# The opening of a fused convolution and SwiGLU kernel: one operation for the taps' second part, late passes one chunk earlier, other places for loads

## The chip, the cores and the metric

The kernel runs on one core of one Trainium2 chip. The metric is the device time of one execution in microseconds (us), the median of three runs. All other times are us from the start of the profiled span unless they are marked ns. Engines are named as in the profile: PE (TensorE, matmuls; PEld are its weight loads), DVE (VectorE), ACT (ScalarE), POOL (GpSimd), SP (SyncE, whose queue issues most transfers). A small q behind an engine's name marks its sequencer, which issues transfers.

## The reference

A causal convolution over the sequence, 7 taps for each of 8 heads (the taps are a softmax of `weight`), then a SwiGLU block on its result. Everything is float32 in and out.

```python
B, S, D = 8, 4096, 192          # x; H = 8 heads of 24 channels, K = 7 taps, Dff = 1536
w = exp(weight - max(weight, -1)); w = w / (sum(w, -1) + 1e-9)
conv[b, s, h, :] = sum over k of w[h, k] * x_padded[b, s + k, h, :]     # 6 zeros ahead
g   = conv @ w_gate             # 192 x 1536
val = conv @ w_val              # 192 x 1536
out = (g * sigmoid(g) * val) @ w_out        # 1536 x 192
```

## The kernel before

**Tiling.** The 32768 tokens are 64 blocks of 512 tokens (`TB`); two blocks make a pair, 32 pairs in all. A block goes through the SwiGLU part in 12 chunks of 128 hidden columns (`NCH`). A chunk's first half is 3 steps of 2 matmuls: `gate` on the lower 64 rows of the array (line 558), `val` on the upper 64 rows (559), side by side. Then ACT makes silu of `gate` (563) and DVE multiplies it with `val` to h (565). PSUM holds two buffers of gate (chunk 2 of block 0 uses a third, the buffer called run), and three of val, so val of chunk j waits for h of chunk j-3. The second half, `acc` += h times w_out (570), lags one block: its matmuls stand between the first halves of the next block, 4 or 6 units of two matmuls a chunk. Chunks are counted through: block 0 has chunks 0 to 11, block 1 has 12 to 23, pair 1 begins at chunk 24.

**The convolution of pair 1 and later** is done by ACT, DVE and POOL in three groups a pair: group 0 (channels 0 to 127 of the first block), group 1 (channels 128 to 191 of both blocks), group 2 (channels 0 to 127 of the second block). Each group's steps have places by chunk: `turn`, DVE's transposition (line 114, squares sqA or sqB to xtA or xtB); `start`, ACT's first product into PSUM (`run`, 485); `acts`, ACT products (478); `dves`, DVE multiply-and-add (495, the last gives aD); `pool`, POOL products (500) and sums (507); `join`, the sum of all parts to xc (513); `swap`, two transfers that exchange the halves of xc to xs (461, 462). A chunk reads xc and xs. A step of a place stands, on every engine's queue, behind that chunk's own work. Engines work their queues strictly in that order. `PLAN["opening"]` (line 17) gives these places for pair 1 as (turn, start, acts, dves, pool, join, swap), one tuple a group.

**The convolution of pair 0** is done by PE, as matmuls of x with banded matrices. The taps are made first: line 273 is the exponential, `turned` the rotated taps, `norm` the reciprocal of their sum. `left` holds the normed taps as two float16 parts: part 0 is rounded (289), part 1 is what the rounding left (292: the taps in float32 as `full`; 293: `full` minus part 0). Four matmuls (337: hiA, loA, hiC, loC) repeat the two parts over the rows, DVE cuts them to bands T (345). x is cast to float16 by ACT (windows 0 to 2) and POOL (windows 3 to 5) at line 244. Then block 0 is convolved (361), folded (420 to 424), gathered (414) and copied to three operands D0, D1, D2 (427 to 431), one for each of a chunk's three steps. Block 1 is convolved in three late passes of 48 matmuls, put between the chunks of block 0: `lateA(0)`, `lateA(1)` and `lateC`. They read x16p, which POOL casts at line 247. Their results go to foldA1 and foldC1 by ACT and are exchanged by transfers (669) to swapA1 and swapC1; block 1 (chunk 12 and on) reads all of them. `spread_taps` (435 to 439) puts the taps, in three parts that POOL makes (lines 323 to 327), on the partitions for the other engines (wn); it uses the masks `mask` and `own`.

**Queues.** POOL's queue issues the weight transfers w_sb in three lots (chunks 0 to 3, 4 to 7, 8 to 11), gate and val apart (169), between its other work. SP's queue takes the taps, x, the squares (103), the exchanges, the swaps and the output (600), in program order; an instruction that waits holds all behind it. `mark` (455) puts an empty instruction on SP's queue that waits for a matmul, and a later matmul waits for it.

**Places of the loads of squares.** `emit_load(q, part, half)`: parts 2 and 3 are sqB, parts 0 and 1 sqA. For pair 1, sqA comes in two halves at chunks 5 and 9; for pair 2 the parts come at chunks 16 (part 2), 17 (part 3), 20 (part 0) and 22 (part 1).

Of the kernel before, what the change touches and what calls it, by code (L numbers as in the profile page):

```python
# [15 lines left out]
    load=((2, -47), (3, -40), (0, -34), (1, -28)),  # L16
    opening=(
# [3 lines left out]
    ),  # L21
    gate=2, val=3, lead=4, third=(2,),
# [4 lines left out]
def kernel(  # L27
# [9 lines left out]
    nc = tc.nc  # L37
    fp32 = mybir.dt.float32
    fp16 = mybir.dt.float16
    int32 = mybir.dt.int32  # L40
    AF = mybir.ActivationFunctionType
    ALU = mybir.AluOpType
    AX = mybir.AxisListType

    B, S, D = x.shape
    H, K = weight.shape
    NT = B * S
    Dff = moe_w_gate.shape[1]
    P = 128
    DB = D - P  # L50
# [12 lines left out]
    const_pool = ctx.enter_context(tc.tile_pool(name="const", bufs=1))  # L63
# [63 lines left out]
    HALF, STEP, W, NW = TB // 2, 85, 96, 6  # L127
    ROWS, LOADED = 94, 96
# [14 lines left out]
    RT = 8 * H  # L143
    taps = const_pool.tile([H, K], fp32, tag="taps", name="taps")
    nc.sync.dma_start(out=taps, in_=weight)
    x_sb = xpool.tile([P, 2, NW, D], fp32, tag="x_sb", name="x_sb", bufs=1)
# [49 lines left out]
    def where(out, t, bits):  # L196
# [16 lines left out]
        out=plain, in_=plain, pattern=[[-32, 4], [-1, grp]],  # L213
# [5 lines left out]
    mask = const_pool.tile([RT, D], fp16, tag="mask", name="mask")  # L219
    nc.gpsimd.memset(mask, 0.0)  # L220
    nc.gpsimd.affine_select(
        out=mask[:, :].rearrange("r (h c) -> r h c", h=H),
# [1 line left out]
        pattern=[[-8, H], [0, grp]],  # L224
        compare_op=ALU.not_equal, fill=1.0, base=0, channel_multiplier=1,
    )
    own = const_pool.tile([RT, P], fp16, tag="own", name="own")
    nc.gpsimd.tensor_copy(
        own[:, :].rearrange("h (t c) -> h t c", t=2),
        mask[:, P:D].unsqueeze(1).to_broadcast([RT, 2, DB]),  # L230
    )
    load_w(0, 4, 0)
    load_w(0, 4, 1)

# [1 line left out]
    x16 = xpool.tile([P, NW, D + 8], fp16, tag="x16", name="x16", bufs=1)  # L236
# [4 lines left out]
        return t.rearrange("p n (h t c) -> p n h t c", t=2, c=grp)[:, :, :, e, :]  # L241

    def cast(copy, lo, hi):
        copy(x16[0:ROWS, lo:hi, 0:D], x_sb[0:ROWS, 0, lo:hi, :])

    def cast_parity(copy, e):
        copy(parity(x16p[0:ROWS, e, :, :], e), parity(x_sb[0:ROWS, 1, :, :], e))


    wmax, wsum, norm = (const_pool.tile([RT, 1], fp32, tag=n, name=n) for n in ("wmax", "wsum", "norm"))  # L250
# [29 lines left out]
    nc.vector.reciprocal(norm, wsum)  # L280

    REP = -(-ROWS // 8)
    full = const_pool.tile([RT, 8], fp32, tag="full", name="full")
    left = const_pool.tile([RT, 2, REP, 8], fp16, tag="left", name="left")

    def repeated(t):
        return t[:, :].unsqueeze(1).to_broadcast([RT, REP, 8])
# [1 line left out]
    nc.vector.tensor_tensor(  # L289
        left[:, 0, :, :], repeated(turned), norm.unsqueeze(1).to_broadcast([RT, REP, 8]), op=ALU.mult  # L290
    )
    nc.vector.tensor_tensor(full, turned, norm.to_broadcast([RT, 8]), op=ALU.mult)
    nc.vector.tensor_tensor(left[:, 1, :, :], repeated(full), left[:, 0, :, :], op=ALU.subtract)
    left = left[:, :, :, :].rearrange("r i n m -> r i (n m)")

    sync_after(nc.sync.nop(), spinning, "block 1's x behind the first weights")
# [4 lines left out]
            emit_load(1, part, None)  # L301
    nc.scalar.activation(two, one, AF.Silu)
    cast(nc.scalar.copy, 0, 3)
    cast(nc.gpsimd.tensor_copy, 3, NW)

    def place(k):
        lo, hi, at = ((0, DB, 0), (DB, 96, 0), (0, 32, 32), (32, 96, 0))[k]
        nc.gpsimd.tensor_copy(
            spread[:, k, :, at : at + hi - lo], plain[:, lo:hi].unsqueeze(1).to_broadcast([P, 2, hi - lo])
        )  # L310
# [4 lines left out]
    load_w(4, 8, 1)  # L315
    place(2)
    place(3)
    for b in range(2):
        load_w(8, NCH, b)

    parts = const_pool.tile([RT, 3, K], fp16, tag="parts", name="parts")
    raw, rest = (const_pool.tile([RT, K], fp32, tag=n, name=n) for n in ("raw", "rest"))
    nc.gpsimd.tensor_tensor(raw, soft[:, 0:K], norm.to_broadcast([RT, K]), op=ALU.mult)
    nc.gpsimd.tensor_copy(parts[:, 0, :], raw)
    nc.gpsimd.tensor_tensor(rest, raw, parts[:, 0, :], op=ALU.subtract)
    nc.gpsimd.tensor_copy(parts[:, 1, :], rest)
    nc.gpsimd.tensor_tensor(parts[:, 2, :], rest, parts[:, 1, :], op=ALU.subtract)

# [109 lines left out]

    for e in range(2):
        cast_parity(nc.gpsimd.tensor_copy, e)

    foldA1, swapA1 = (
        const_pool.tile([P, 2, TH], fp16, tag=n, name=n) for n in ("foldA1", "swapA1")
# [181 lines left out]
    def at_chunk(c, f):  # L627
        todo.setdefault(c, []).append(f)
# [33 lines left out]
    def lateA(g):  # L662
        if g == 0:
            late_sum()
        halves(g, late["sum"][:, g, :])
# [20 lines left out]
        at_chunk(2 * NCH, blank)  # L686

    late = {}
    at_chunk(3, lambda: lateA(0))
    at_chunk(4, lambda: spread_taps(tpool.tile([P, TB], fp32, tag="run", name="run")))  # L690
    at_chunk(4, lambda: lateA(1))
    at_chunk(4, outA)
    at_chunk(7, lateC)
    if n_pairs > 1:
        for half, c in enumerate((5, 9)):
            for part in (0, 1):
                at_chunk(c, lambda part=part, half=half: emit_load(1, part, half))

# [3 lines left out]
    for q in range(2, n_pairs):  # L702
        base = 2 * NCH * q
        for part, c in PLAN["load"]:
            c = {2: 16, 3: 17, 0: 20, 1: 22}[part] if q == 2 else base + c
            at_chunk(c, lambda q=q, part=part: emit_load(q, part))
        for g in range(3):
            c = base + PLAN["start"][g]
            plan_group(
                q, g, c + PLAN["turn"], c, [c + o for o in PLAN["acts"][g]],  # L710
                [c + o for o in PLAN["dves"][: 4 - PLAN["npool"][g]]],
                c + PLAN["pool"], c + PLAN["join"],
                c + PLAN["swap"][g],
            )
# [7 lines left out]
    for n in range(2 * n_pairs):  # L722
        block = Block(n)
        for j in range(NCH):
            src, units = before if j < NCH - lead // 4 else block, late_start.get(at, 4)
            if n == 0:
                src, units = block, 0
            elif n == 2 * n_pairs - 1 and src is block:
                units = 0
            los, his = src.second(units)  # L730
            half = src.done // (2 * NCH) - 1 if units and src.done % (2 * NCH) == 0 else None
            if n == 0 and j < 2:
                if j == 0:
                    for k in range(2):
                        for i in range(2):
                            block.first(i, (k,))
                block.first(j, (2,))
            elif half is None:
                block.first(j)
            for lo, hi in zip(los, his):  # L740
                lo()
                hi()
            if half is not None:
                src.evacuate(half)
                block.first(j)
            block.gate(j)
            if half is not None:
                src.store(half)
            for f in todo.pop(at, ()):
                f()  # L750
            at += 1
        before = block
# [61 lines left out]
```

## Time and profile before

| | |
|---|---|
| median of 3 runs | 774.21 us (773.54 to 774.4) |
| the profiled execution | 773.69 us, of which the span from first to last instruction 771.9 us |
| mean granted clock of PE | 0.999 |
| busy share PE, PEld, DVE, ACT, POOL | 99%, 76%, 85%, 86%, 86% |
| instructions | 28286 |
| transfers | 67.28 MB, mean 87 GB/s |

In a row of a timeline stand start, length, engine, line, operation, the output and the input with their shapes, how many instructions are merged in the row, and in brackets how long the engine had been idle before and what ended it. A row of a chain of waits has start, length and the work (or "issue", time in which nothing that the profile shows was waited for). A row of transfers has output and input, the issuing queue, how many, KB each, and us from issue to landing. Matmuls overlap: their lengths are latencies, and the distance of their starts is what they cost PE.

### The profile page before, as it was taken

The numbers are of one execution on the slowest core, as the hardware profiler recorded it, in microseconds if no ns is written. First come the engines' busy times: TensorE is split into PE (matmuls) and PEld (weight loads), VectorE is DVE, ScalarE is ACT, GpSimd is POOL, SyncE is SP. The second block draws the span as 40 slices with busy tenths as digits, with TensorE's granted clock in tenths as the row PEclk, the third lists the DMA queues.
The fourth block names the chain that finished last, engine by engine and source line by source line (L and its number), as shares of the span: only waits on it lengthen the run. The fifth ranks groups of instructions, "written<-read, shape, count | busy, mean of one in ns | idle before, by whom it ended". The sixth has DMA issues, their size and how long they took to land.

```text
span 771.9 us, 28286 instructions
## 1 busy us (share of the span) xinstructions
PE 764.1 (99%) x11035; PEld 588.3 (76%) x11035; DVE 659.2 (85%) x1045; ACT 660.6 (86%) x1188; POOL 667.6 (86%) x654
## 2 busy tenths in 40 slices
PE   8899999999999999999999999999999999999998
PEld 4777777777777777777777777777777777777776
DVE  6888888889888888888888888888888888888875
ACT  6888888888888888888888888888888888888875
POOL 6899988888988889988889888899888899888850
PEclk9999999999999999999999999999999999999999
DMA  9544344433444443444334444334443434444211
GB/s 162 103 85 85 82 97 84 94 86 80 88 87 95 84 86 87 87 88 95 85 79 86 95 84 95 86 83 87 83 98 82 89 85 88 88 90 91 61 47 53
DMA packets 255287, 67.28 MB, mean 87 GB/s; under 512 B 207920, under 2 KB 255152, under 8 KB 255152
## 3 DMA queue, kind: packets, MB, share of 16 engines
q1 hardware_dynamic: 252048, 63.48, 39.3%
q0 software_dynamic: 2800, 1.77, 1.6%
q8 instruction: 86, 1.41, 0.8%
q14 instruction: 49, 0.40, 0.2%
q10 hardware_dynamic: 304, 0.22, 0.1%
HBM read 29.65 MB, written 25.17 MB: 71 GB/s over the span
## 4 chain that ended last, share of the span: by engine, by line
PE 95%; POOL 3%; DVE 1%; issue 1%; DMA 0%; ACT 0%; SPq 0%; POOLq 0%; DVEq 0%; ACTq 0%
PE val L559 49%; PE acc L570 34%; PE gate L558 11%; POOL t L507 1%; POOL t L500 1%; DMA xs<-xc 0%; POOL xc L513 0%; PE acc L765 0%; ACT silu L563 0%; PE D L414 0%; PE idle L264 0%; PE acc L361 0%; PE val L765 0%; PE run L765 0%; PE hiA L361 0%
## 5 line engine op out<-in xcount | busy, mean ns | idle before, releaser
L565 DVE TENSOR_TENSOR h<-silu,val 128x512 f16<-128x512 f16 x768 | 508.8, 679 | 103.7 <-ACT silu L563 74.3
L563 ACT ACTIVATE silu<-gate 128x512 f16<-128x512 f32 x768 | 452.7, 594 | 80.1 <-PE gate L558 73.8
L570 PE MATMUL acc<-wo_sb,h 64*128 64x192 f16 x6048 | 471.7, 243 | 1.0 <-SPq L455 1.0
L507 POOL TENSOR_TENSOR t<-t,t 128x512 f32<-128x512 f32 x310 | 393.3, 1269 | 61.6 <-ACT t L478 39.2
L570 PEld LDWEIGHTS <-h 64*128 64x128 f16 x6048 | 397.2, 94 | 62.9 <-SPq L455 1.3
L558 PE MATMUL gate<-xc,w_sb 64*128 64x512 f16 x1116 | 409.7, 376 | 0.0
L559 PE MATMUL val<-xc,w_sb 64*128 64x512 f16 x1116 | 409.7, 376 | 0.0
L558 PE MATMUL gate<-xs,w_sb 64*128 64x512 f16 x1116 | 360.2, 376 | 0.7 <-DMA xs<-xc 0.7
L559 PE MATMUL val<-xs,w_sb 64*128 64x512 f16 x1116 | 360.0, 376 | 0.4 <-DMA xs<-xc 0.4
L559 PEld LDWEIGHTS <-w_sb 64*128 64x128 f16 x2340 | 212.0, 94 | 105.1 <-issue 3.6
L558 PEld LDWEIGHTS <-w_sb 64*128 64x128 f16 x2340 | 212.1, 94 | 5.1 <-issue 2.3
L513 POOL TENSOR_TENSOR xc<-t,aD 128x512 f16<-128x512 f32 x93 | 118.1, 1270 | 7.3
L500 POOL TENSOR_SCALAR t<-xtA,wn 128x512 f32<-128x512 f32 x155 | 105.7, 692 | 0.0
L478 ACT ACTIVATE t<-xtA,wn 128x512 f32<-128x512 f32 x124 | 88.4, 713 | 0.0
L608 ACT COPY o<-acc 128x384 f32<-128x384 f32 x126 | 60.3, 478 | 19.7 <-PE acc L570 6.5
L500 POOL TENSOR_SCALAR t<-xtB,wn 128x512 f32<-128x512 f32 x62 | 42.1, 691 | 6.4 <-DVE xtB L114 6.4
L495 DVE SCALAR_TENSOR_TENSOR aD<-xtA,wn,run 128x512 f32<-128x512 f32 x62 | 45.9, 740 | 0.0
L478 ACT ACTIVATE t<-xtB,wn 128x512 f32<-128x512 f32 x62 | 44.2, 713 | 0.0
L485 ACT ACTIVATE run<-xtA,wn 128x512 f32<-128x512 f32 x62 | 42.5, 686 | 0.5 <-DVE aD L495 0.5
L114 DVE STREAM_TRANSPOSE xtA<-sqA 128x544 f32<-128x544 f32 (+1 forms) x48 | 34.6, 720 | 0.0
L495 DVE SCALAR_TENSOR_TENSOR run<-xtA,wn,run 128x512 f32<-128x512 f32 x31 | 23.2, 749 | 0.0
L495 DVE SCALAR_TENSOR_TENSOR run<-xtB,wn,run 128x512 f32<-128x512 f32 x31 | 23.2, 748 | 0.0
(111 smaller groups left out, 182.9 us busy)
## 6 DMA issues: line engine op xcount, KB each, us to landing
out_dram<-o SPq DMA_DIRECT2D x127, 192.0 KB, 2.0
sqA<-in_x_dram SPq DMA_DIRECT2D x92, 132.0 KB, 3.1
xs<-xc SPq DMA_DIRECT2D x186, 64.0 KB, 2.0
sqB<-in_x_dram SPq DMA_DIRECT2D x96, 68.0 KB, 2.3
headA<-in_x_dram SPq DMA_DIRECT2D x28, 128.0 KB, 2.7
headB<-in_x_dram SPq DMA_DIRECT2D x14, 68.0 KB, 2.5
headB<-in_x_dram SPq DMA_DIRECT2D x14, 64.0 KB, 2.1
x_sb<-in_x_dram SPq DMA_DIRECT2D x3, 216.0 KB, 3.3
```

Of the source, the lines that this page charges most:

```text
L478: mul(parts[-1], *self.tap(k))
L485: nc.scalar.mul(self.aD, *self.tap(0))
L495: nc.vector.scalar_tensor_tensor(out=self.aD, in0=v, scalar=s, in1=run, op0=ALU.mult, op1=ALU.add)
L500: self.product(k, lambda t, v, s: nc.gpsimd.tensor_scalar(t, v, scalar1=s, scalar2=1.0, op0=ALU.mult, op1=ALU.mult), self.parts)
L507: nc.gpsimd.tensor_tensor(self.parts[0], self.parts[0], t, op=ALU.add)
L513: nc.gpsimd.tensor_tensor(xc, self.parts[0], self.aD, op=ALU.add)
L558: nc.tensor.matmul(g, w[0:DB, ca, f], a[0:DB, :], start=(i == 0), stop=(i == 2))
L559: nc.tensor.matmul(v, w[DB:P, cb, f], b[DB:P, :], start=(i == 0), stop=(i == 2))
L563: nc.scalar.activation(s, self.g.pop(j), AF.Silu)
L565: nc.vector.tensor_tensor(h, s, self.v.pop(j), op=ALU.mult)
L570: ins = nc.tensor.matmul(acc, self.h[j][r, ts(s, P)], wo_r[r, j, :], start=first and j == 0, stop=not first and j == NCH - 1, skip_group_c ...
L608: nc.scalar.copy(self.o[:, 2 * half : 2 * half + 2, :], self.acc[:, :, 0:D])
```

## The change

- The taps' second part: `full` is gone; one scalar_tensor_tensor computes `turned * norm - left[0]`.
- POOL's cast of windows 3 to 5 waits for that operation.
- `own` moves on POOL from ahead of the first weight transfers to behind the last `place`, ahead of the third lot of weights. The five operations that make `parts` move behind POOL's casts of x16p.
- Chunks 0 and 1: the steps on D0 of both chunks still come first; then chunk 0's steps on D1 and D2, then chunk 1's. Before, D1 came for both chunks ahead of D2.
- The late passes stand at chunks 2, 3 and 6 instead of 3, 4 and 7, with the copies and exchanges behind them. `spread_taps` stays at 4.
- Group 1 of pair 1: `start` at chunk 7 instead of 6, the first DVE step at 9 instead of 8.
- Loads of squares: pair 1's sqA first half at chunk 4 instead of 5; pair 2's at 11, 12, 20 and 21 instead of 16, 17, 20 and 22.

No matmul is added or removed; DVE has one operation less.

```diff
-        (5, 6, (9, 12), (8, 12), 6, 13, 16),
+        (5, 7, (9, 12), (9, 12), 6, 13, 16),
...
-    own = const_pool.tile([RT, P], fp16, tag="own", name="own")
-    nc.gpsimd.tensor_copy(
-        own[:, :].rearrange("h (t c) -> h t c", t=2),
-        mask[:, P:D].unsqueeze(1).to_broadcast([RT, 2, DB]),
-    )
     load_w(0, 4, 0)
     load_w(0, 4, 1)
...
-    nc.vector.tensor_tensor(full, turned, norm.to_broadcast([RT, 8]), op=ALU.mult)
-    nc.vector.tensor_tensor(left[:, 1, :, :], repeated(full), left[:, 0, :, :], op=ALU.subtract)
+    left_second = nc.vector.scalar_tensor_tensor(
+        out=left[:, 1, :, :], in0=repeated(turned), scalar=norm, in1=left[:, 0, :, :],
+        op0=ALU.mult, op1=ALU.subtract,
+    )
...
-    cast(nc.gpsimd.tensor_copy, 3, NW)
+    sync_after(cast(nc.gpsimd.tensor_copy, 3, NW), left_second, "not beside the taps")
...
     place(3)
+    own = const_pool.tile([RT, P], fp16, tag="own", name="own")
+    nc.gpsimd.tensor_copy(
+        own[:, :].rearrange("h (t c) -> h t c", t=2),
+        mask[:, P:D].unsqueeze(1).to_broadcast([RT, 2, DB]),
+    )
     for b in range(2):
         load_w(8, NCH, b)
...
     for e in range(2):
         cast_parity(nc.gpsimd.tensor_copy, e)
 
+    parts = const_pool.tile([RT, 3, K], fp16, tag="parts", name="parts")
+    raw, rest = (const_pool.tile([RT, K], fp32, tag=n, name=n) for n in ("raw", "rest"))
+    nc.gpsimd.tensor_tensor(raw, soft[:, 0:K], norm.to_broadcast([RT, K]), op=ALU.mult)
+    nc.gpsimd.tensor_copy(parts[:, 0, :], raw)
+    nc.gpsimd.tensor_tensor(rest, raw, parts[:, 0, :], op=ALU.subtract)
+    nc.gpsimd.tensor_copy(parts[:, 1, :], rest)
+    nc.gpsimd.tensor_tensor(parts[:, 2, :], rest, parts[:, 1, :], op=ALU.subtract)
...
-    at_chunk(3, lambda: lateA(0))
+    at_chunk(2, lambda: lateA(0))
     at_chunk(4, lambda: spread_taps(tpool.tile([P, TB], fp32, tag="run", name="run")))
-    at_chunk(4, lambda: lateA(1))
-    at_chunk(4, outA)
-    at_chunk(7, lateC)
+    at_chunk(3, lambda: lateA(1))
+    at_chunk(3, outA)
+    at_chunk(6, lateC)
     if n_pairs > 1:
-        for half, c in enumerate((5, 9)):
+        for half, c in enumerate((4, 9)):
...
-            c = {2: 16, 3: 17, 0: 20, 1: 22}[part] if q == 2 else base + c
+            c = {2: 11, 3: 12, 0: 20, 1: 21}[part] if q == 2 else base + c
...
                 if j == 0:
-                    for k in range(2):
-                        for i in range(2):
-                            block.first(i, (k,))
-                block.first(j, (2,))
+                    block.first(0, (0,))
+                    block.first(1, (0,))
+                block.first(j, (1, 2))
```

More of the change, by code (lines that the diff above doesn't have):

```diff
@@ L243, in cast @@
     def cast(copy, lo, hi):
-        copy(x16[0:ROWS, lo:hi, 0:D], x_sb[0:ROWS, 0, lo:hi, :])
+        return copy(x16[0:ROWS, lo:hi, 0:D], x_sb[0:ROWS, 0, lo:hi, :])
     def cast_parity(copy, e):
@@ L282 @@
     REP = -(-ROWS // 8)
-    full = const_pool.tile([RT, 8], fp32, tag="full", name="full")
     left = const_pool.tile([RT, 2, REP, 8], fp16, tag="left", name="left")
@@ L317 @@
     place(3)
+    own = const_pool.tile([RT, P], fp16, tag="own", name="own")
[3 more added lines that the diff above has]
+    )
     for b in range(2):
         load_w(8, NCH, b)
[L321 to L327, printed above, removed]
     T = const_pool.tile([P, 2, H, W], fp16, tag="T", name="T")
```

## The prediction

> **What bounds the kernel now.** I read the stages first (busy time of each engine by stretch), then the chain of waits of the first 56 us, then the rows of the opening, engine by engine.
>
> ```profile
> 12.00:14.00 2.00, 1.67 (x42) 0.71 (x42) 1.79 (x3) 1.56 (x4) 0.18 (x1) 1.00 1.30 186
> 18.00:20.00 2.00, 1.54 (x58) 0.84 (x54) 1.30 (x3) 1.51 (x4) 1.36 (x2) 1.00 0.49 88
> 32.00:34.00 2.00, 1.10 (x24) 1.03 (x26) 0.87 (x2) 1.05 (x2) 1.92 (x3) 1.00 0.46 75
> 50.00:690.00 640.00, 640.00 (x9172) 495.93 (x9170) 557.76 (x872) 560.82 (x1010) 579.19 (x549) 1.00 0.42 88
> ```
>
> The columns: stretch, length, then busy us of PE, PEld, DVE, ACT and POOL, granted clock, DMA share, GB/s. From 50 to 690 us PE is never idle, and the change touches nothing there. So it can gain only what it brings forward the moment from which PE is saturated. PE's holes, 0.33 at 12-14, 0.46 at 18-20 and 0.90 at 32-34, lie in the opening. Which of them count is told by the chain of waits (start, length, what):
>
> ```profile
> 17.72 0.75 DVE xtB L114
> 23.75 0.72 ACT t L478
> 24.61 1.27 POOL t L507
> 32.73 1.27 POOL xc L513
> 45.84 3.82 DMA xs<-xc
> ```
>
> POOL works without a hole from 24.61, when ACT's product at chunk 12 (23.75) sets group 1's sum free, to the xc of group 0 at 34.00. Chunk 24, the first of token pair 1, needs that xc and its swapped copy xs. So **the time of chunk 24 is set by POOL, POOL's by chunk 12, and chunk 12's by how fast block 0 (chunks 0 to 11) runs.** Holes of PE in chunks 14 to 23 (32-34) are no gain by themselves. The chain's next step, xs at 45.84, is for chunk 36, a transfer that the change leaves in its place.
>
> **The front (L289 to the first gate matmul).**
>
> ```profile
> 2.87 0.36 POOL L228 COPY own<-mask 64x128 f16<-64x128 f16 x1
> 4.05 0.64 POOL L169 DMA_DIRECT2D w_sb<-in_moe_w_val_dram  x1
> 4.68 0.68 POOL L244 CAST x<-x_sb 94x576 f16<-94x576 f32 x1
> ...
> 3.85 0.25 DVE L289 TENSOR_TENSOR left<-turned,norm 64x96 f16<-64x96 f32 x1
> 4.02 0.61 DVE L292 TENSOR_TENSOR full<-turned,norm 64x8 f32<-64x8 f32 x1
> 4.67 0.80 DVE L293 TENSOR_TENSOR left<-full,left 64x96 f16<-64x96 f32 x1
> ...
> 4.31 0.55 PE L337 MATMUL hiA<-pick,left 64*94 64x384 f16 x1
> 5.53 0.55 PE L337 MATMUL loA<-pick,left 64*94 64x384 f16 x1 [0.67 <-DVE left L293]
> 5.88 0.52 PE L337 MATMUL hiC<-pick,left 64*94 64x384 f16 x1
> 6.65 1.05 PE L361 MATMUL hiA<-T,x 94*32 94x85 f16 x48
> 10.15 0.39 PE L558 MATMUL gate<-D,w_sb 64*128 64x512 f16 x1
> ...
> w_sb<-in_moe_w_val_dram POOLq DMA_DIRECT2D x1, 192.0 KB, 5.5
> ```
>
> Removed: L292 (0.61) and L293 (0.80), done at 5.47. Added: one operation over 64x96 that waits for L289 (4.10). Nearest rows: L289, same size, 0.25; L293, same size beside POOL's cast, 0.80. I take 0.3, since the cast now waits behind it: done at 4.45 (4.94 at the upper end). loA then follows hiA at PE's own pace (5.88-5.53 = 0.35): 4.31+0.35 = 4.66 instead of 5.53, **-0.87** (at the upper end 4.98, -0.55). loA, hiC, loC and the convolution from 6.65 on follow in PE's order and move as much. POOL's cast is not late: it began at 4.68 behind the two weight transfers, and own (0.36), which stood ahead of them, is now behind; with the new wait it begins at about 4.5 (5.0 at the upper end, harmless, since the convolution would begin at 5.8 to 6.1). Queued behind the cast on POOL are place, own and the later weight transfers: they come 0.2 earlier to 0.3 later.
>
> The first gate and val matmuls also need the val weights: 4.05+5.5 = 9.55. Without own ahead they are issued 0.36 earlier, so 9.2, or still 9.55 if the transfer engines were the limit. First matmuls: **10.15 to 9.28** (9.6 at worst).
>
> The Trainium skill ("SBUF — State Buffer", Who interferes with whom) says that a VectorE operation with two SBUF inputs is blocked by a GpSimd operation that reads SBUF, not by one that only writes. L293 agrees: it ends 0.11 after the cast that began with it (5.36). L292, 64x8 and still 0.61, does not: only a transfer's issue (4.05 to 4.69) lies beside it. By the rule the new operation costs about 0.3, by L292's row up to 0.6 more.
>
> **Block 0.**
>
> ```profile
> 10.74 0.37 PE L558 MATMUL gate<-D,w_sb 64*128 64x512 f16 x1
> 10.95 0.37 PE L558 MATMUL gate<-D,w_sb 64*128 64x512 f16 x1
> 12.95 0.37 PE L559 MATMUL val<-D,w_sb 64*128 64x512 f16 x1 [0.33 <-DVE h L565]
> 13.69 0.65 PE L361 MATMUL acc<-T,x16p 94*32 94x85 f16 x48
> 14.27 0.39 PE L558 MATMUL gate<-D,w_sb 64*128 64x512 f16 x1
> 15.63 0.39 PE L558 MATMUL gate<-D,w_sb 64*128 64x512 f16 x1
> 19.75 0.37 PE L558 MATMUL gate<-D,w_sb 64*128 64x512 f16 x1 [0.46 <-ACT silu L563]
> ...
> 11.58 1.57 ACT L563 ACTIVATE silu<-gate 128x512 f16<-128x512 f32 x3 [0.74 <-PE val L559]
> 18.49 0.69 ACT L485 ACTIVATE run<-xtB,wn 128x512 f32<-128x512 f32 x1 [0.76 <-DVE xtB L114]
> ...
> 12.21 2.70 DVE L565 TENSOR_TENSOR h<-silu,val 128x512 f16<-128x512 f16 x4 [1.22 <-ACT silu L563]
> ...
> 9.89 1.26 POOL L247 CAST x16p<-x_sb 94x576 f16<-94x576 f32 x2
> ...
> 4.39 2.64 SPq L103 DMA_DIRECT2D sqB<-in_x_dram  x4
> sqB<-in_x_dram SPq DMA_DIRECT2D x1, 68.0 KB, 8.3
> ```
>
> *Order of chunks 0 and 1.* The matmuls on D1 (10.74 before, about 9.87 now) are followed by those on D2 of chunk 0, not by D1 of chunk 1: silu 0 comes one matmul step earlier. A step is 0.216 (10.74 to 10.95), a chunk three of them, 0.65. Silu 0: 11.58-0.87-0.22 = 10.49, h 0 at 11.12, and val of chunk 3, which waits for h 0 (its PSUM buffer), 12.95 to 11.86.
>
> *Late passes one chunk earlier.* The first (48 matmuls, 14.27-13.69 = 0.58 of PE) stood behind chunk 3 and now falls into the hole ahead of it: from 9.87 seven steps end chunk 2 at 11.38, the pass lies at 11.38-11.96, chunk 3 at 11.96 (from 12.95: -1.0). It needs x16p, cast by 11.15 before; five operations on parts move from ahead of that cast to behind it and only own (0.36) comes ahead, so it is earlier, and even its old time would do. The parts themselves are first wanted by the tap matmuls after chunk 4, some 2.5 later. Chunk 3 (0.65) and the second pass (0.58) put chunk 4 at 13.2 (from 14.27: -1.1); with no pass behind it, only the taps (15.63-14.27-0.65-0.58 = 0.13), chunk 5 is at 13.98 (from 15.63: **-1.7**). VectorE, 0.67 a chunk (12.21, four in 2.70), gets to h 5 at 15.5 and to xtB, whose place at chunk 5 is kept, at 16.15 (from 17.72: **-1.6**). Its input sqB is there: the last of its four loads is issued before 7.03 and lands 8.3 after its issue, so before 15.4.
>
> *ACT's run one chunk later.* Before, ACT stood 0.76 for xtB and then did run (18.49, 0.69) ahead of silu 7 (about 19.1); PE's chunk 9 waited for that (19.75). Now silu 7 is ahead of run: it comes at 16.7, run at 17.2, which xtB (done 16.9) no longer delays. Chunk 9 moves to 17.3 (-2.4). The product that run feeds is one chunk later too (place 8 to 9); it is wanted by aD at chunk 12 only. From there VectorE's 0.67 a chunk and its two extra operations hold the pace: chunk 12 at 20.2, ACT's product at 21.5 (from 23.75: -2.2), POOL's last sums and xc as much. **Block 0 with the front: -2.2 at POOL.**
>
> **Loads and swaps on SP.**
>
> ```profile
> 30.20 2.51 SPq L103 DMA_DIRECT2D sqB<-in_x_dram  x2
> 34.02 0.76 SPq L461 DMA_DIRECT2D xs<-xc  x1
> ...
> 32.90 0.50 PE L570 MATMUL acc<-wo_sb,h 64*128 64x192 f16 x8 [0.98 <-SPq L455]
> 37.25 0.37 PE L558 MATMUL gate<-xs,w_sb 64*128 64x512 f16 x1 [0.67 <-DMA xs<-xc]
> ...
> xs<-xc SPq DMA_DIRECT2D x1, 64.0 KB, 2.5
> xs<-xc SPq DMA_DIRECT2D x186, 64.0 KB, 2.0
> ```
>
> Pair 2's sqB loads (chunks 16, 17) held SP until 32.71, with the mark that PE's acc waits for behind them: PE's 0.98. At chunks 11 and 12 they are issued when SP is free, before group 1's swap, so that wait goes. What is late next: PE reaches chunk 24 some 3 us earlier and finds xs 2.2 earlier, so its wait there grows from 0.67 to 0.67+0.98 = about 1.65. That 0.98 is thus worth nothing in the sum. xs of group 0 is issued when xc is done, 34.02-2.2 = 31.8, its second half 0.8 later, and lands 2.5 after that: 35.1 where it was 37.3. The part moved from chunk 22 to 21 is now issued right behind xs, the one of chunk 20 is out 1.5 earlier; an xs took 2.5 here, 3.82 at chunk 36 (in the chain), 2.0 in the median of all 186: -0.5 to +1.3 on the landing, taken as 0, since both neighbours move. Chunk 24, and with it everything to the end: **-2.2**. Chunk 36 keeps its wait.
>
> **Sum.** Front -0.87, order -0.22, late passes -0.5 and ACT's run -0.6 as they arrive at POOL: -2.2. The profiled execution took 773.69 (span 771.9, 1.8 around it), 0.5 under the median of 774.21; it would come to 771.5, the median to **772.0**. Ends: a slow new operation (+0.3), weights at 9.55 (+0.3), xs late (+1.3) against xs early (-0.5) and operands D1 and D2 ready when the first matmuls start (-0.5: D1's matmul came 0.59 after the first, of which two steps are work at most): -0.3 to -3.2, or 773.9 to 771.0.
>
> **Rivals.**
> *The transfers bound the opening (no change or little).* sqA, the folded blocks' exchanges and pair 2's sqB now start some 2 us earlier, while the transfer engines are still full of weights (DMA share 1.30 at 12-14). If chunk 12's exchanged operands, or xs at chunk 24, then keep nearly their old time, as xs at 45.84 did with 3.82, 1.0 to 1.3 of the 2.2 is lost: 773.1. For it: the share, and the 3.82. Against: at 18-20 the share is down to 0.49. Chance 0.20.
>
> *The clock comes late (the other side).* The convolution's 48 matmuls took 1.05 at 6.65, the late pass's 48 took 0.65 at 13.69: PE got its full clock between. At half clock every us of PE's work after 9.28 takes two. If, with PE's rhythm changed, the full clock came at 13.7 instead of ahead of 10.74, (13.7-9.28)/2 = 2.2 would be lost, all of the gain; at 17 it is 3.9, the kernel 1.7 slower: 775.9. Against: PE has fewer holes than before ahead of 9.28. Chance of slower 0.09.
> The Trainium skill ("TensorE: Matmul & The Clock Gate", Part 1) has the full clock follow one sustained busy window of about 3.4 us. By that rule the closed hole at 4.66-5.53 would bring it earlier, and the convolution faster; the gate matmuls would still wait for weights at 9.2, so 771.7 at best; no run here shows that yet.
>
> *The change does not shorten the taps.* If POOL's transfer issue blocks VectorE as at 4.02, the new operation ends near 5.0 and the front gives 0.5: 772.4, still faster; inside the forecast; with the weights at 9.55 and xs late too it falls under what can be measured, 0.04.
>
> **Chances.** What a measurement of this kernel can tell from no change is about 0.2%, 1.55 us. Forecast (-1.55 to -3.2) 0.67; transfers bound the opening or the front stays long, both with a gain under 1.55, 0.24; slower 0.09. The range 770.9 to 773.8 takes in the forecast, a little more for an earlier clock, and most of the second case.
>
> **What would show it.** Right: one tap operation of 0.25-0.35 at 4.1 and loA at 4.7; first gate matmul at 9.2-9.4; no hole ahead of chunk 3; xtB near 16.1; ACT's product at chunk 12 near 21.5; POOL's xc of group 0 done at 31.8; no PE wait on SP near 30; a PE wait of 1.2 to 2 for xs at chunk 24. Wrong: gate matmuls at 9.6 or later, the late pass waiting for x16p, chunk 12 waiting for its exchanged operands, or xs landing more than 3 us after its issue.

## The result and the profile after

The changed kernel takes 772.5 us (median of 13 runs, 772.04 to 774.22), the kernel before beside it 774.0 (13 runs, 773.08 to 774.77): ratio 0.9982, 95% interval 0.9974 to 0.9991, or 1.5 us faster (0.7 to 2.0). The profiled execution took 772.73 with a span of 771.0, so the two profiles are 0.96 apart: the one of before lay 0.3 under its median, the one of after 0.2 above. The forecast was 772.0, the range 770.9 to 773.8.

Busy time by stretch of the changed kernel (columns as in the prediction):

```profile
14.00:16.00 2.00, 2.00 (x32) 0.91 (x20) 1.17 (x2) 1.75 (x4) 0.00 (x0) 1.00 0.96 92
16.00:18.00 2.00, 2.00 (x64) 1.05 (x61) 2.00 (x5) 1.43 (x4) 0.33 (x1) 1.00 1.51 178
18.00:20.00 2.00, 1.69 (x16) 0.69 (x14) 1.38 (x3) 2.00 (x5) 1.92 (x3) 1.00 1.22 207
50.00:690.00 640.00, 639.00 (x9152) 414.07 (x9154) 556.77 (x871) 557.11 (x1009) 580.31 (x548) 1.00 0.41 88
```

Two rows are new. From 50 us on PE has a hole of 1.00, where it had none. And at 18-20 us the transfer engines are at 1.22 (before 0.49), after a hole of their own at 14-16 (0.96, before 1.49). The groups of PE's waits from 8 to 75 us (total, times, longest) and PE's own rows tell where:

```profile
PE acc L571 <- SPq L456: 1.8, 2, 1.0
PE gate L559 <- ACT silu L564: 0.3, 1, 0.3
PE gate L559 <- DMA swapC<-foldC: 0.2, 1, 0.2
PE val L560 <- DMA swapC<-foldC: 0.2, 1, 0.2
```

```profile
4.13 0.31 DVE L286 SCALAR_TENSOR_TENSOR left<-turned,norm,left 64x96 f16<-64x96 f32 x1
...
4.65 0.52 PE L330 MATMUL loA<-pick,left 64*94 64x384 f16 x1
9.40 0.60 PE L559 MATMUL gate<-D,w_sb 64*128 64x512 f16 x1
9.80 0.63 PE L559 MATMUL gate<-D,w_sb 64*128 64x512 f16 x1
12.12 0.65 PE L354 MATMUL acc<-T,x16p 94*32 94x85 f16 x48
12.70 0.39 PE L559 MATMUL gate<-D,w_sb 64*128 64x512 f16 x1
21.05 0.27 PE L559 MATMUL gate<-foldA,w_sb 64*128 64x256 f16 x1
21.96 0.27 PE L559 MATMUL gate<-swapC,w_sb 64*128 64x256 f16 x1 [0.19 <-DMA swapC<-foldC]
22.40 0.27 PE L560 MATMUL val<-swapC,w_sb 64*128 64x256 f16 x1 [0.17 <-DMA swapC<-foldC]
27.15 1.16 PE L571 MATMUL acc<-wo_sb,h 64*128 64x192 f16 x24 [0.82 <-SPq L456]
36.28 0.38 PE L559 MATMUL gate<-xc,w_sb 64*128 64x512 f16 x1
57.02 0.51 PE L571 MATMUL acc<-wo_sb,h 64*128 64x192 f16 x8 [1.00 <-SPq L456]
57.36 0.38 PE L559 MATMUL gate<-xc,w_sb 64*128 64x512 f16 x1
```

The front came as forecast. Chunk 3 was brought forward by 0.25 only (12.95 to 12.70): the first steps, 9.40 and 9.80, still ran at half pace (0.40 apart, where a step took 0.22 later). Chunk 12 (21.05) reached its last step at once and stood there for swapC, first for one half, then for the other. So chunk 13 starts at 22.40, where it was 23.05. ACT's product of chunk 12 and POOL's xc follow, 1.0 earlier:

```profile
22.76 0.71 ACT L479 ACTIVATE t<-xtB,wn 128x512 f32<-128x512 f32 x1
...
31.76 1.27 POOL L514 TENSOR_TENSOR xc<-t,aD 128x512 f16<-128x512 f32 x1
```

From there PE wins more than POOL. xs landed at 35.68 (before 37.37); chunk 25, the first after the wait at chunk 24, starts at 36.28 (before 38.01, -1.73), and with the wait at chunk 36 gone too, chunk 37 at 48.02 (before 50.27, -2.25). Then it is lost again in two places. At chunk 38 the weight loads for `acc` wait for a mark on SP, and chunk 38 takes 1.32 instead of 0.98: 0.34 lost. At chunk 44 PE waits 1.00 for another mark, and chunk 45 starts at 57.36 (before 58.09), -0.73. The rows of the wait at chunk 38 and of SP ahead of chunk 45:

```profile
49.98 0.28 PEld L571 LDWEIGHTS <-h 64*128 64x128 f16 x8 [0.48 <-SPq L456]
...
55.43 0.47 SPq L462 DMA_DIRECT2D xs<-xc  x1
55.95 0.89 SPq L463 DMA_DIRECT2D xs<-xc  x1
```

SP's two rows are the swap of pair 2's group 0 (place: chunk 42), which waits for POOL's xc (54.13 to 55.40). The mark of chunk 43 stands behind it on SP's queue. In the same way the mark of chunk 37 stands behind the swap of pair 2's group 1 (place: chunk 35; its issue ended at 49.79). In the kernel before PE came to chunk 44 later, so that the same mark cost nothing, but only just. The second half of that swap and `acc` of chunk 44 there:

```profile
56.90 0.59 SPq L462 DMA_DIRECT2D xs<-xc  x1
...
57.76 0.52 PE L570 MATMUL acc<-wo_sb,h 64*128 64x192 f16 x6
```

In the changed kernel `acc` started 0.18 after the issue of the second half ended (56.84 to 57.02). With the same 0.18 the mark was ready at about 57.67 in the kernel before (an estimate), 0.1 ahead of its use.

### The profile page after: what moved, and what is told of

Its sections match the earlier page's. It is cut to its first block, busy times and chain, and to the rows that moved or that the text cites. A ratio compares the mean times of both kernels' runs of the same rounds, so it can differ in the third digit from the quotient of the medians.

```text
span 771.0 us, 28286 instructions
## 1 busy us (share of the span) xinstructions
PE 764.5 (99%) x11035; PEld 497.7 (65%) x11035; DVE 658.0 (85%) x1044; ACT 658.1 (85%) x1188; POOL 669.0 (87%) x654
## 4 chain that ended last, share of the span: by engine, by line
PE 97%; SPq 1%; POOL 1%; ACT 0%; issue 0%; DVE 0%; POOLq 0%
PE gate L559 60%; PE acc L571 32%; PE val L560 3%; SPq L103 1%; POOL t L508 0%; PE idle L259 0%; PE acc L765 0%; PE D L407 0%; PE acc L354 0%; ACT silu L564 0%; POOL xc L514 0%; SPq L670 0%; PE val L765 0%; PE run L765 0%; PE hiA L354 0%
## 5 line engine op out<-in xcount | busy, mean ns | idle before, releaser
L571 PEld LDWEIGHTS <-h 64*128 64x128 f16 x6048 | 275.7, 94 | 143.1 <-SPq L456 3.1
L571 PE MATMUL acc<-wo_sb,h 64*128 64x192 f16 x6048 | 356.8, 243 | 1.8 <-SPq L456 1.8
```

What stands on the lines that cost most here:

```text
L571: ins = nc.tensor.matmul(acc, self.h[j][r, ts(s, P)], wo_r[r, j, :], start=first and j == 0, stop=not first and j == NCH - 1, skip_group_c ...
```

## The experiments

All are edits of the changed kernel, but for the taps alone, an edit of the kernel before; none leaves work out. Each ran against the kernel before on its own chip (774.16 to 774.35 there). "Chunk 13", "ACT", "xc", "chunk 45" are from the profiles: the start of chunk 13, of ACT's product at chunk 12, the end of POOL's xc of pair 1's group 0, the start of chunk 45.

| run | median us | against before, interval | chunk 13 | ACT | xc | chunk 45 | span |
|---|---|---|---|---|---|---|---|
| before | 774.0 | | 23.05 | 23.75 | 34.00 | 58.09 | 771.9 |
| changed | 772.5 | 0.9974-0.9991 | 22.40 | 22.76 | 33.03 | 57.36 | 771.0 |
| changed, again | 772.68 | 0.9969-0.9987 | 22.36 | 22.67 | 32.94 | 57.31 | 770.9 |
| swap behind the mark | 771.7 | 0.9950-0.9975 | 22.43 | 22.77 | 33.03 | 56.16 | 769.9 |
| w_out first | 772.24 | 0.9962-0.9983 | 21.56 | 22.25 | 32.51 | 56.81 | 770.4 |
| both | 771.04 | 0.9950-0.9975 | 21.60 | 22.29 | 32.55 | 55.75 | 769.5 |
| both, run at its old place | 771.71 | 0.9955-0.9980 | 21.74 | 22.43 | 32.70 | 55.88 | 769.7 |
| late passes old | 773.21 | 0.9975-0.9993 | 23.11 | 23.73 | 33.98 | 58.01 | 771.6 |
| loads old | 772.85 | 0.9972-0.9990 | 21.98 | 22.61 | 32.87 | 57.13 | 770.7 |
| run at its old place | 772.72 | 0.9973-0.9990 | 22.22 | 22.57 | 32.84 | 57.36 | 770.9 |
| front alone | 773.75 | 0.9986-1.0004 | 22.42 | 23.12 | 33.37 | 58.55 | 772.2 |
| taps alone | 773.8 | 0.9985-1.0003 | 23.38 | 24.02 | 34.28 | 58.50 | 772.3 |

Two things hold in all twelve rows: xc ends 10.25 to 10.27 after ACT's product, and the span ends 713.5 to 713.8 after chunk 45 starts. So POOL follows chunk 12, and whatever happens ahead of chunk 45 counts only by when chunk 45 starts. A difference of start times is not always the edit's work, however: the first profile of the changed kernel and that of both edits caught the half pace at the first steps, and the others for one step at most.

**The swap behind the mark** (the wait at chunk 44).

```diff
-                c + PLAN["swap"][g],
+                c + PLAN["swap"][g] + (q == 2 and g == 0),
```

> The changed kernel, with the swap of pair 2's group 0 one place later (chunk 43 instead of 42), so that the mark of chunk 43 stands ahead of it on SP's queue. Theory 'second gate': in the changed kernel PE had won 2.25 us by chunk 37, and lost 1.0 of it at chunk 44, where it waited 1.00 for a mark on SP that stood behind that swap, which waited for POOL's xc. Then here the 1.00 goes, chunk 45 starts at about 56.4 instead of 57.36, and the time is 0.7 to 1.0 us under the changed kernel's (about 771.6). Rival 'pace': what PE wins ahead of chunk 44 has to be given back anyway, to ACT, DVE and POOL, which have their own pace in every pair; then the 1.00 comes back as other waits between chunks 44 and 60 and the time stays within 0.3 us of the changed kernel's.

Measured: 771.7, chunk 45 at 56.16. Its rows around chunk 44 (chunks 44 and 45, then the first half of the swap):

```profile
55.19 0.38 PE L559 MATMUL gate<-xc,w_sb 64*128 64x512 f16 x1
56.16 0.38 PE L559 MATMUL gate<-xc,w_sb 64*128 64x512 f16 x1
...
55.57 0.47 SPq L462 DMA_DIRECT2D xs<-xc  x1
```

xc ends at 33.03 as in the changed kernel, chunk 44 starts within 0.02 of it (55.21), and chunk 45 follows after 0.97, one chunk, with no wait; no later wait takes it back. So the wait at chunk 44 cost the change 1.0 to 1.2 by the profiles (0.8 to 1.0 by the medians), and "pace" is out. The smaller wait at chunk 38 is still there (chunk 38 takes 1.43).

**w_out first** (chunk 12's exchanged operands). The one transfer of w_out is issued on POOL ahead of the casts of x16p:

```diff
+    nc.gpsimd.dma_start(out=wo_r, in_=moe_w_out.rearrange("(c p) d -> p c d", p=P))
     for e in range(2):
         cast_parity(nc.gpsimd.tensor_copy, e)
...
-    nc.gpsimd.dma_start(out=wo_r, in_=moe_w_out.rearrange("(c p) d -> p c d", p=P))
```

> The changed kernel, with the transfer of w_out issued ahead of POOL's casts of x16p instead of behind parts (about 9.9 instead of 12.46). Theory 'transfers': chunk 12 waited 0.19 and 0.17 for swapC, which landed at 21.92 and 22.36, hardly earlier than before the change, because x of block 1, the casts and the w_out transfer had become later and the transfer engines were busier at 16 to 20 us (1.51 and 1.22 against 1.02 and 0.49). With w_out out of the way swapC lands 0.5 to 0.8 earlier, ACT's product at chunk 12 comes at about 22.1 (from 22.76), POOL's xc of group 0 ends at about 32.4 (from 33.03), and the time is 0.6 less, since chunk 44 follows POOL. Rival 'SP': swapC is late because SP issues the halves of sqA and swapC one behind the other (1.44 and 1.25 us of issue), which w_out does not touch: no wait at chunk 12 changes by more than 0.1 and the time stays within 0.3.

Measured: 772.24, ACT at 22.25, xc 32.51, chunk 45 at 56.81 (-0.55). Busy time by stretch of this run, and then SP's issue of swapC, the last step of chunk 12 and the first of chunk 13:

```profile
14.00:16.00 2.00, 2.00 (x20) 0.80 (x17) 0.75 (x3) 1.74 (x3) 0.00 (x0) 1.00 1.63 195
...
18.00:20.00 2.00, 1.69 (x15) 0.68 (x13) 1.38 (x3) 2.00 (x5) 1.92 (x3) 1.00 0.61 97
```

```profile
18.89 1.11 SPq L669 DMA_DIRECT2D swapC<-foldC  x2
...
21.45 0.27 PE L560 MATMUL gate<-swapC,w_sb 64*128 64x256 f16 x1
21.56 0.27 PE L560 MATMUL gate<-foldA,w_sb 64*128 64x256 f16 x1
```

The hole at 14-16 is filled (92 to 195 GB/s), w_out lands at 18.62 instead of 20.47, swapC at 21.27 instead of 22.36, and chunk 12 goes through without a wait. "Transfers" holds. The second profile of the changed kernel is the closest partner, for chunk 12 starts at 20.91 in both: chunk 13 then starts at 21.56 here and at 22.36 there. The medians alone would not show it: they are 0.26 to 0.44 apart, less than the 0.6 expected, and the intervals overlap. SP's issues of swapC became shorter too (1.90 to 1.11), though nothing on SP was changed, so that what "SP" took for a cause followed from the same backlog. With POOL 0.52 earlier, the wait at chunk 44 stays (0.88) and chunk 45 moves with POOL, by 0.55.

**Both edits.**

> The changed kernel with both edits: the transfer of w_out ahead of the casts of x16p, and the swap of pair 2's group 0 behind the mark of chunk 43. Alone, the first brought chunk 45 from 57.36 to 56.81 and the second to 56.16. Theory 'chain': the first brings POOL 0.5 forward (its xc of pair 1's group 0 ends at 32.5 instead of 33.03), and without the wait at chunk 44 PE keeps what it wins at chunks 24 and 36: chunk 45 at 55.6, the time 0.4 to 0.6 under that of the second edit alone (about 771.2). Rival 'pace': POOL, DVE and ACT had just kept up after the second edit, and another wait (for xs at chunk 48, or for silu) takes the 0.5 back: 771.6 to 771.8.

Measured: 771.04, the fastest of all, chunk 45 at 55.75: 0.41 ahead of the swap alone. PE's waits that are left from 8 to 75 us:

```profile
PE val L561 <- DMA xs<-xc: 0.6, 2, 0.3
PE gate L560 <- DMA xs<-xc: 0.3, 1, 0.3
PE gate L560 <- ACT silu L565: 0.3, 1, 0.3
```

No mark and no swapC among them; what PE still waits for is mostly xs. "Chain" holds. The 0.41 is won at chunk 38: chunk 37 starts as with the swap alone (47.93 and 47.90), but chunk 38 takes 0.98 here and 1.43 there, since POOL's xc, the swap of group 1 behind it and the mark behind that are earlier. The first steps ran at half pace in this profile too (9.41 to 10.24 for the three steps of chunk 0), and it is the fastest nevertheless.

**Late passes at 3, 4 and 7.**

```diff
-    at_chunk(2, lambda: lateA(0))
+    at_chunk(3, lambda: lateA(0))
...
-    at_chunk(3, lambda: lateA(1))
-    at_chunk(3, outA)
-    at_chunk(6, lateC)
+    at_chunk(4, lambda: lateA(1))
+    at_chunk(4, outA)
+    at_chunk(7, lateC)
```

> The changed kernel with the late passes at their old places (chunks 3, 4 and 7). My prediction gave them 0.5 of the gain at POOL, and the hole ahead of chunk 3. Theory 'chain': the hole ahead of chunk 3 is back (0.3 to 0.5), chunk 5 starts some 0.6 later than in the changed kernel, the exchange of block 1 is issued a chunk later and chunk 12 waits longer for it: ACT's product at chunk 12 and POOL's xc come 0.5 to 1.0 later, and the end with them: 0.5 to 1.0 us slower than the changed kernel. Rival 'DVE paces block 0': VectorE at 0.67 a chunk fills block 0 in either order, so that chunk 12 moves by less than 0.2 and the time with it.

Measured: 773.21, ACT 23.73, xc 33.98, both 0.95 or more later than in the changed kernel and level with the kernel before; chunk 45 at 58.01, +0.65. The medians are 0.5 to 0.7 apart, with intervals that overlap. The hole ahead of chunk 3 is back in part (`gate` at 11.57, `val` at 12.05). PE's wait at chunk 12:

```profile
22.93 0.27 PE L559 MATMUL gate<-swapC,w_sb 64*128 64x256 f16 x1 [0.59 <-DMA swapC<-foldC]
```

Beside the other parts POOL's gain hangs on the late passes, because they bring the exchange forward: swapA's issue starts at 16.20 here and 14.76 in the changed kernel, swapC's at 20.71 and 19.20, and the first half of swapC lands 0.97 later (22.89 and 21.92). How much of this is theirs alone stays open: chunk 4 also waited 0.39 for the second lot of weights here, which landed at 14.10 (13.41 and 13.93 in the changed kernel).

**Loads of squares at their old places** (pair 1's first half at chunk 5; pair 2's at 16, 17, 20, 22).

> The changed kernel with the loads of squares at their old places (pair 1's sqA at chunk 5, pair 2's at 16, 17, 20 and 22). Theory 'chain': PE's wait of 0.82 for a mark at chunk 16 goes and the old one of 0.98 near chunk 20 comes back; neither decides, since chunk 24 waits for POOL's xc and xs. swapC may be issued up to 0.5 earlier, since no part of sqB stands near it on SP. The time stays within 0.4 us of the changed kernel's. Rival 'loads carry the gain': xs at chunks 24 and 36 landed 2.3 and 3.2 us after issue in the changed kernel against 3.2 and 3.8 before because the squares were loaded earlier; then with the old places xs lands late again, PE waits at chunk 24 (0.5 or more) and 36 (0.4), and if no later gate levels it the time is back near the old kernel's (about 773.5).

Measured: 772.85, chunk 45 at 57.13. The wait at chunk 16 is gone, one of 0.4 near chunk 20 is back, xs of chunk 24 lands at 35.59 (35.68 in the changed kernel). PE waits 0.60 for it, as "loads carry the gain" had it, but chunk 25 starts level with the changed kernel (36.23 and 36.28), and the time stays within the 0.4 of "chain". The places of the loads carry nothing of the gain that could be seen.

**Group 1's run at its old place** (`(5, 6, (9, 12), (8, 12), 6, 13, 16)`), in the changed kernel and then with both edits above.

> The changed kernel with group 1's first ACT product at chunk 6 and its first DVE step at chunk 8, as before the change. My prediction gave the move 0.6 at POOL. Theory 'chain': silu of chunk 7 stands behind that product and its wait for xtB again, chunk 9 starts 0.6 or more later than 18.4, chunk 12 and POOL follow, and the time is 0.6 over the changed kernel's. Rival 'transfers': chunks 7 to 11 come later, but chunk 12 waits for swapC until 22.4 in either case, so ACT's product at chunk 12 stays at 22.7 to 22.9 and the time within 0.3.

> The changed kernel with both edits (w_out's transfer first, the swap behind the mark) and with group 1's first ACT product at chunk 6 and first DVE step at chunk 8, as before the change. In the changed kernel itself moving these two back cost nothing (772.72 us, POOL's xc even 0.19 earlier), where I had forecast 0.6. Two theories. 'Hidden': the move is worth 0.6, but chunk 12 waits for swapC and covers it; then here, where chunk 12 no longer waits (it began at 20.95 and went through in 0.65), chunk 12 comes 0.5 later, ACT's product there at 22.8 instead of 22.29, POOL's xc of group 0 ends at 33.0 instead of 32.55, and the time is 0.4 to 0.6 above 771.04. 'Worthless': with xtB done earlier ACT no longer stands before its product at chunk 6, and what remains is one product (0.69) that has to be done in block 0 either way; then chunk 12 and POOL stay within 0.2 and the time within 0.3.

Measured: 772.72, and 771.71 with both edits. In the first, chunk 9 started at 18.34 (18.37 in the first profile of the changed kernel); in the second, chunk 12 started at 21.09 against 20.95, and chunk 45 came 0.13 later. That looks like "worthless", but the profiles differ ahead of the move, since their partners had been caught with the half pace: chunk 5 starts at 14.22 and 14.33 here and at 14.74 and 14.64 there. So the stretch from chunk 5 to chunk 12 has to be compared. It takes 6.76 in both runs with the old place (6.76 or 6.77 in the kernel before, the front alone and the taps alone too), and 6.31 or 6.32 in all six profiles with the new place and the early late passes. Chunk 7, ACT and chunk 9 with the old place, in the changed kernel; then chunk 7 and its silu with the new place, in the changed kernel's second profile:

```profile
16.35 0.39 PE L559 MATMUL gate<-D,w_sb 64*128 64x512 f16 x1
17.08 0.69 ACT L486 ACTIVATE run<-xtB,wn 128x512 f32<-128x512 f32 x1 [0.24 <-DVE xtB L114]
17.71 1.06 ACT L564 ACTIVATE silu<-gate 128x512 f16<-128x512 f32 x2
18.34 0.37 PE L559 MATMUL gate<-D,w_sb 64*128 64x512 f16 x1 [0.52 <-ACT silu L564]
...
16.72 0.39 PE L559 MATMUL gate<-D,w_sb 64*128 64x512 f16 x1
17.58 0.60 ACT L564 ACTIVATE silu<-gate 128x512 f16<-128x512 f32 x1 [0.37 <-PE val L560]
```

Silu 7 starts 1.36 after its chunk with run ahead of it, 0.86 without. So the mechanism of "hidden" holds, at 0.45 instead of 0.6. In the changed kernel the wait for swapC covers it, as "transfers" had it (ACT's product at 22.57). With both edits it is there, less the 0.31 by which chunk 5 was ahead, which leaves the 0.14 seen at chunk 12. The medians of the last pair, 771.71 and 771.04, come from two chips and lie 0.67 apart (0.48 if each is taken against the kernel before on its chip); this fits, but their intervals overlap.

**The front alone, and the taps alone.** The front alone has the taps' one operation, the cast behind it, own and parts moved, and all else as before the change; the taps alone leave own and parts too.

> The kernel before, with one part of the change alone: the taps' second part in one operation, and POOL's cast behind it. Everything else, own and parts too, stands at its old place. My prediction gave this part 0.87 at loA, of which the val weights (landed 9.60 before) leave 0.5: first gate matmul at 9.6. Theory 'chain': chunk 12, ACT's product there and POOL's xc come 0.5 earlier, and so does the time: 0.4 to 0.7 under the kernel before. Rival 'transfers': swapC lands at 22.1 and 22.5 as before, chunk 12 (22.40 before, one step each at those times) cannot start its second operand earlier, and the time moves by less than 0.3.

> As the run with the taps alone, and own and parts moved as in the change; the order of chunks 0 and 1, the late passes, group 1's places and the loads are those of the kernel before. Theory 'chain': the val weights come 0.4 earlier, the first gate matmul at 9.3, so the time is 0.2 to 0.4 under the run with the taps alone. Rival 'transfers': parts stand ahead of the w_out transfer on POOL, which is issued some 1.2 later and lands near 20 instead of 18.2; the exchange of block 1 lands behind it, chunk 12 waits for swapC until 22.5 or later, and the time is that of the kernel before (within 0.3) or above the run with the taps alone.

Measured: 773.8 and 773.75, neither told from the kernel before by its interval. With the taps alone the convolution's 48 matmuls took 0.88 (1.05 before) and the first gate matmul came at 8.26, and yet nothing was gained. Both fit an early full pace in this profile (loA took 0.37, where it took 0.52 in the changed kernel) and are no gain of the taps. PE's rows:

```profile
5.50 0.88 PE L362 MATMUL hiA<-T,x 94*32 94x85 f16 x48
...
8.26 0.39 PE L559 MATMUL gate<-D,w_sb 64*128 64x512 f16 x1
...
9.62 0.39 PE L560 MATMUL val<-D,w_sb 64*128 64x512 f16 x1 [0.97 <-DMA w_sb<-in_moe_w_val_dram]
...
14.53 0.39 PE L560 MATMUL val<-D,w_sb 64*128 64x512 f16 x1 [0.73 <-DMA w_sb<-in_moe_w_val_dram]
```

The weights of chunks 0 and 4 hold it, whatever the pace; the second lot's val part landed at 14.48, where it was 12.83 in the kernel before, from the same issue time (6.32 and 6.38). POOL ended later than before (34.28). Both theories missed here: the brake was a transfer, but the weights, not swapC (landed 23.34, after its own late issue). Why the second lot came so late is open: it landed between 13.41 and 14.10 in the profiles with own moved. With own out of the way (front alone, where it landed at 13.63) POOL came 0.63 earlier than in the kernel before (xc 33.37), as "chain" had it, and chunk 12 did not wait for swapC (landed 22.27). Chunk 45 is still 0.46 later than before, which neither theory had. SP's and PE's rows:

```profile
56.28 1.74 SPq L463 DMA_DIRECT2D xs<-xc  x1
58.23 1.06 SPq L103 DMA_DIRECT2D sqA<-in_x_dram  x2
...
58.21 0.50 PE L571 MATMUL acc<-wo_sb,h 64*128 64x192 f16 x8 [0.92 <-SPq L456]
```

The mark at chunk 44 again, this time behind a swap whose issue took 1.74 (0.89 in the changed kernel, 0.59 with both edits). In all runs with that wait chunk 45 starts 0.52 to 0.54 after this issue ends.

**The changed kernel again** (the clock).

> The changed kernel as it is, beside the others on one chip. In its first profile PE had its full clock from 10.80 on, in that of the run with the swap behind the mark, whose first 40 chunks are the same work, from 9.26; chunk 11 came 0.47 apart, chunk 13 at 22.40 and 22.43. Theory 'transfers': whatever the clock does here, chunk 13 starts between 22.2 and 22.6, swapC lands at 22.2 to 22.5, POOL's xc of group 0 ends at 32.9 to 33.1 and chunk 45 starts at 57.2 to 57.5; the time is 772.3 to 772.9, some 1.5 above the best of the others. Rival 'clock': with the full clock a us earlier or later chunk 45 moves by half of that.

Measured: 772.68, xc 32.94, chunk 45 at 57.31. The first steps of this profile:

```profile
9.15 0.39 PE L559 MATMUL gate<-D,w_sb 64*128 64x512 f16 x1
9.38 0.38 PE L559 MATMUL gate<-D,w_sb 64*128 64x512 f16 x1
...
22.35 0.27 PE L560 MATMUL val<-swapC,w_sb 64*128 64x256 f16 x1 [0.21 <-DMA swapC<-foldC]
```

PE had its full pace from the first step on, and chunk 13 starts at 22.36, 0.04 from the profile with the half pace. "Clock" falls, since swapC sets chunk 13 in either case. The other profiles bear this out: in all six in which chunk 12 waited for the first half of swapC, its silu started 0.34 or 0.35 after that half had landed, whether chunk 12 had started at 20.54 or at 21.62.

## Why the prediction was right, and where it was wrong

**Right in sign and in range, and too large:** -2.2 forecast, -1.5 by the medians, -0.96 by the profiles. In the prediction's own classes this is just outside the forecast (-1.55 to -3.2) and in the case where the transfers take a part of the gain.

- *The front.* Tap operation 0.31 (0.3 taken), loA 4.65 (4.66), first gate 9.40 and 9.15 (9.28; 9.2 to 9.4 named). Right in place. But the taps alone are worth nothing (34.28 at POOL); the step that lets the gain through is the one costed in half a sentence, own moved off the way of the weights: with it POOL gains 0.63 (one profile each, and parts moved with it).
- *The order of chunks 0 and 1.* Silu 0 came 1.15 to 1.26 after the first gate matmul in the profiles with full pace (before 1.43): 0.17 to 0.28 for the 0.22 taken. In the first profile the half pace hid it (11.15). No run moved the order alone, so what it is worth further on is not shown.
- *Late passes.* No hole ahead of chunk 3, as said (11.98 in the second profile, 11.96 forecast). Their 0.5 was too small: up to 0.95 at POOL and 0.65 at chunk 45, by the exchange that they bring forward, which I had not put into the sum.
- *ACT's run, -0.6.* The mechanism was right: silu 7 stood behind run. Its size was 0.45 at chunk 12. But as a term of the sum it failed: in the changed kernel chunk 12 waits for swapC, which covers it, so nothing of it reached POOL.
- *Chunk 12 at 20.2, ACT's product at 21.5.* Measured 20.91 to 21.05 and 22.67 to 22.76. In the product, 0.4 of the 1.2 is the wait for swapC (product 1.71 and 1.76 after chunk 12's start, 1.34 with both edits), the rest chunks that came later, by the forecast's own count. In the changed kernel the wait alone decides: with the swap behind the mark, the same work up to there, chunk 12 started at 20.58 and the product came at 22.77 all the same. Here the first rival stepped in as described, chunk 12's exchanged operands keeping nearly their old time: 22.36 against 22.52. It priced the loss at 1.0 to 1.3 of the 2.2, which by the profiles is what came (1.2); its 773.1 is 0.6 above the median. That the sizes agree is in part luck: the rival took its price from an xs that landed 3.82 after its issue, and w_out moved ahead brings back 0.4 to 0.5 at POOL. What I missed is why. I called parts behind the casts harmless, since the first that reads them comes some 2.5 later, and did not follow the queue that they stand in: behind them on POOL is the transfer of w_out. Block 1's x came 1.87 later (9.88, before 8.01), the casts waited for it and ended at 11.28 (before 11.15; "earlier" was forecast), parts followed, and w_out was issued 1.35 later and landed 2.3 later, with swapA and swapC behind it. No run moved parts alone, but the taps alone, with parts at their old place, issued w_out at 11.04, and the front alone at 12.12.
- *Loads.* The wait of 0.98 went and is worth nothing, right. That no wait on SP would be left near 30 was wrong (0.82 at 27.15), and harmless, as chunk 24 waits for POOL.
- *xs.* Taken as 0, measured about -0.7 beyond POOL: 2.3 and 2.1 us from issue to landing for the two halves, against 3.2 and 2.5. The wait of 1.65 forecast at chunk 24 did not show, since PE came there 1.15 and 1.76 earlier and not 3: chunk 24 takes 1.24 and 1.71 in the two profiles, before 1.82. Chunk 36, which was to keep its wait, takes 0.97 and 1.32, before 1.51, so only the first profile lost it whole.
- *"Chunk 24, and with it everything to the end."* Wrong, and the costliest step. PE gained 2.25 by chunk 37, nearly the forecast, then lost 0.34 at chunk 38 and 1.0 to 1.2 at chunk 44, both behind marks that had not been the last to be ready before. The row from 50 to 690 us, PE never idle, was read as "the change touches nothing there"; it says only that the marks were ready in time, not by how much, and at chunk 44 it was 0.1. Since these marks stand behind swaps that wait for POOL's xc, the end moved with POOL after all: xc came 0.97 earlier and the time is 0.96 less, by the profiles.
- *The early end of the range.* The -0.5 for D1 and D2 does not follow from its rows: 0.59 less two steps of 0.216 is 0.16. It was no part of the forecast.

The second rival, the late clock, was there in the first profile (half pace until about 10.7) and cost nothing at the end, since the wait for swapC covers it too. The third did not happen.

## What to carry to other kernels

A stretch with no idle time is saturated at its present start only: before a gain is carried to the end, look for the marks and swaps in it and how long each was ready ahead of its use, because what comes earlier by 2 us meets all that came 1 us early. Small operations moved on a queue that issues transfers move every transfer behind them, so follow that queue to its next large transfer and to whoever lands behind it. Parts of a change that are covered by the same wait do not add, and taking one back then shows nothing: ACT's run, worth 0.45 at chunk 12, cost nothing to move back as long as chunk 12 waited for swapC. Where start times of two profiles are compared, take the stretch from the last point that the edit cannot have moved.

## What the hardware showed that was not expected

While the main part of w_out was on its way the exchange stood still. Packets by queue in the changed kernel from 16 to 18 us (packets, MB, share):

```profile
q0 software_dynamic: 886, 0.34, 147.7%
```

From 18 to 20 us, with little of w_out left:

```profile
q1 hardware_dynamic: 1748, 0.33, 84.0%
q0 software_dynamic: 243, 0.09, 37.5%
```

POOL's transfers go by q0, SP's by q1. From 16 to 18 us q1 has no packet, though SP had issued both halves of swapA by 15.92 and sqA from 15.97 on. swapA landed at 20.77, 0.3 after w_out. The Trainium skill ("DMA: Bandwidth & Descriptors", Queues, rings and completion order) says that each transfer engine takes turns between the queues, packet by packet. By that rule swapA would have moved beside w_out; in these two us the trace does not agree. Why SP's queue stood still was not tried.

The moment of the full clock is no property of the kernel: with the same work, steps were 0.40 to 0.43 apart until 10.66 in one profile and 0.23 at 9.15 in the other. The Trainium skill ("TensorE: Matmul & The Clock Gate", Part 1) says that the window that decides is free-running, which the prediction had left out of the rule; the trace agrees, and a closed hole ahead of it promised no earlier clock: with the hole ahead of loA closed in both profiles, the first step at full pace came at 10.95 and at 9.15 (before: 10.15).
